# Moving three scatters to the end of a head pair, and the writing of empty rows into the second pair

## The chip, the cores and the metric

The kernel runs on one core of one Trainium2 chip. The metric is the device time of one execution in microseconds (us); of several executions the median counts.

## The reference

Attention with a hash mask, and then a mixture of experts on its result. For 4 batches, 8 heads, 768 positions and head size 64, queries and keys get a 6-bit bucket from the signs of a projection, and a query sees only the keys of its own bucket:

```python
q_bits = (np.einsum('bhsd,dk->bhsk', q, proj) > 0).astype(np.int64)
mask = q_bucket[:, :, :, None] == k_bucket[:, :, None, :]
scores = np.where(mask, scale * np.matmul(q, k.transpose(0, 1, 3, 2)), -1000000000.0)
attn = softmax(scores)
attn_out = np.matmul(attn, v)
```

The 3072 rows of 512 numbers that come of it go to one of 8 experts each, the one with the largest gate logit; a row's result is its gate weight times `np.maximum(x @ w1[e], 0.0) @ w2[e]`.

## The kernel before

**Stages.** The attention runs over 16 pairs of heads, g = 0 to 15 (four pairs to a batch). In a pair, TensorE makes 12 score tiles of 128 x 768 (line 300 the main product, line 298 one with the low parts of q and k and the mask bits), VectorE takes the row peaks (line 310), ScalarE the exponentials (line 316), and the tiles are transposed: four pairs of tiles by VectorE in 32 x 32 blocks (line 362), after which 16 DMAs put the blocks in their places (line 369, tensors z to pt), the other two on TensorE (line 330). In the next pair TensorE multiplies with v (lines 403 and 417), and lines 458 and 468 bring the result to token rows, xr, with the gate logits beside them. Once a batch is done, `route` finds expert and row number (slot) of each token in small steps, and the rows are scattered to a DRAM tensor `sorted_rows` that has a region for each expert. The experts' matmuls (lines 876, 915, 949) then read regions of that tensor with the load sizes fixed in advance; rows that no token fills must hold an empty row (zeros and a row number out of range), so `fill` writes 512 empty rows to the head of each of the 8 regions, ahead of the scatters.

**Order.** The order of the work is written out by hand: PLAN, NEXT, LAST and HEAD are strings of short step names, and `step` runs them one after the other, for the pairs 1 to 13, 14, 15 and 0. Each engine takes its instructions in that order, in one row per engine. What matters here: G is the projection for the hash bits (line 255), P0 to P7 prepare the next pair's q and k on GpSimd (`split`: P0, P1, P4 and P5 casts, lines 191 to 197; P2, P3, P6 and P7 low parts, lines 199 and 201), B writes the mask bits to DRAM and N reads them back (lines 266 and 271, issued by GpSimd), D0 to D3 are the block transposes, I and U the loads of q, k and v, V0 and V2 the two halves of the product with the block-transposed tiles (line 403, 24 matmuls a half), and C is one scatter.

**Scatters.** `scatter(b, hf)` is a generator for half of a batch: it copies the token numbers (line 584), and then issues three indirect DMAs from GpSimd, one for 128 rows each, with a small memset on a "spacer" ahead of each (lines 586 and 587). Each C in a pair runs it on by one DMA, in the pairs that WHEN names: 7 and 8 for batch 0, 11 and 12 for batch 1, 14 for the first half of batch 2.

**Fills.** `fill(e)` is one DMA of 1156 KB, issued by SP, for region e (line 148). The first six read one row of zeros in SBUF over and over, fills 6 and 7 copy the first region's rows in DRAM. Fills 0 to 3 stand in pair 0, at the steps z0 and z1 (the mask reads for pair 1); one more stands behind the 16 DMAs of the pairs 1, 2, 3 and 4 each (`blocks`, line 372). SP is the queue of all loads: q, k, v, the pt copies, later the weights.

Of the kernel before, what the change touches and what calls it, by code (L numbers as in the profile page):

```python
# [15 lines left out]
B, H, S, D = 4, 8, 768, 64  # L16
# [11 lines left out]
RW = GC + 2  # L28
# [14 lines left out]
FILL = 512  # L43
# [11 lines left out]
def lsh_attention_moe(ctx, tc, qk, qk2, v, proj, wg, w1, w1p, w2, w2p, out):  # L55
# [8 lines left out]
    xs = nc.dram_tensor("sorted_rows", [E * ROW, RW], F32).ap()  # L64
# [72 lines left out]
    C = {}  # L137
# [8 lines left out]
    def fill(e):  # L146

        nc.sync.dma_start(xs[e * ROW:e * ROW + FILL].rearrange("(p j) w -> p j w", p=128),
                          C["empty"][:, 0:1].to_broadcast([128, FILL // 128, RW]) if e < 6 else
                          xs[:FILL].rearrange("(p j) w -> p j w", p=128))  # L150

    def late_consts():
        tri = const.tile([128, 128], BF16, name="tri")
# [182 lines left out]
    def pt_tile(u):  # L336
        if u % 2 == 0:
            if "t" not in PT:
                PT["t"] = wk.tile([128, 4, 4, 2, NT, 32], F32, name="pt", bufs=1)
            PT[u] = PT["t"]  # L340
        elif u not in PT:
            PT[u] = wk.tile([128, 4, 2, 2, NT, 32], F32, name="pq", bufs=1)
        return PT[u]

    def turned(g):

        return 0 if g in (0, NG - 1) else 3 if g == NG - 2 else 4

    ZT = {}
    FILLS = {1: (4,), 2: (5,), 3: (6,), 4: (7,)}  # L350

    def blocks(g, c):

        if g not in ZT:
            ZT[g] = (moe.tile([128, 4, 3, 2 * NT * 32], F32, name="w0") if g == NG - 2 else
                     zp.tile([128, 4, 4, 2 * NT * 32], F32, name=f"z{g % 2}")), []
        z, n = ZT[g]
        n.append(c)
        i = 12 * g + 2 * c
        del PP[i], PP[i + 1]  # L360
        e = EP.pop(i // 2).rearrange("p s h c -> p (s h c)").rearrange("p (k g j) -> p g k j", g=4, j=32)
        nc.vector.transpose(z[:, :, c].rearrange("p g (k i) -> p g k i", i=32), e)  # L362
        if len(n) == turned(g):
            pt = pt_tile(2 * g)[:, :, :turned(g)]
            for h in range(2):
                for k in range(8):
                    x, j, y = k // 4, k // 2 % 2, k % 2
                    a, q = h + 2 * (x ^ y), (h ^ j) + 2 * y
                    nc.sync.dma_start(pt[32 * q:32 * q + 32, a].rearrange("p t s k i -> p (t s k i)"),
                                      z[32 * a:32 * a + 32, q].rearrange("p c x -> p (c x)"))  # L370
            del ZT[g]
            for e in FILLS.get(g, ()):
                fill(e)

    def trans_ev(c, k, vec):

# [356 lines left out]
    P2 = {}  # L733
# [66 lines left out]
    def tokens(n):  # L800
        r, o, c = PH[n]
        IX[n] = moe.tile([128, 4], I32, name="ix", bufs=3)
        t = len(tiles_of(c))
        nc.vector.tensor_copy(IX[n][:, :t], XG[n][:, :t, XG[n].shape[2] - 1].bitcast(I32))
# [204 lines left out]
    def weight_half(op, x):  # L1009
# [28 lines left out]
    PLAN = """  # L1038
        S1 P1 S0 Z1 G R1 S3 T30- Z1 R0 T51- T31- Z1 H T50- R3 Z1 S2 X0 E51v- S4 E31a- P3 T52- E50a- R2 T32- X1 S8 R4 D0
        A2 S5 X3 R5 E32a- M0- E30a- Z2 B S9 X2 R8 E52a- Z2 X4 V1- P4 P0 S6 Z2 D1 S7 R9 Z2 N R6 X8 V0- V2- O1- R7 X5 A1  # L1040
        Z1 X6 X7 I X9 D2 P5 D3 C O0- U Z2 T41 S11 E41a R11 T40 E40a K0- S10 L0- T42 P2 K1- X11 P7 P6 A0 R10 X10 L1-
        E42a C C
    """.split()

    NEXT = """
# [48 lines left out]
    def step(g, w):  # L1094
# [27 lines left out]
        elif op == "D":  # L1122
            if int(x) < turned(n):
                blocks(n, int(x))
# [78 lines left out]
    for g in range(NG):  # L1203
        if g == NG - 2:
            turn.close()
            late["p"] = ctx.enter_context(tc.tile_pool(name="late", bufs=1, side="right", reuse_waits="tile"))
        for w in HEAD if g == 0 else LAST if g == NG - 1 else NEXT if g == NG - 2 else PLAN:
            step(g, w)
            if g == 0 and w in ("z0", "z1"):
                fill(2 * int(w[1]))  # L1210
                fill(2 * int(w[1]) + 1)
            if g == NG - 1 and w == "c1":
                GT[0] = moe.tile([128, 4], F32, name="gate", bufs=3)
                nc.vector.tensor_copy(GT[0][:, :2], XG[0][:, :, GC])
                tokens(0)
# [60 lines left out]
    with tc.If(C["n"] > 0):  # L1276
        with tc.For_i(0, C["n"], 1) as i:
# [16 lines left out]
            p = ps.tile([128, 512], F32, name="t", bufs=2)  # L1294
# [5 lines left out]
            for f in range(8):  # L1300
                p = ps.tile([128, 512], F32, name="t", bufs=2)
# [3 lines left out]
            p = ps.tile([128, 512], F32, name="s", bufs=3)  # L1305
# [35 lines left out]
```

## Time and profile before

| | |
|---|---|
| timed runs | 692.9, 694.75 and 698.5 us; median 694.75 |
| the profiled execution | 690.59 us |
| its span, first to last instruction | 688.8 us |
| TensorE clock granted, mean | 0.994 |
| busy: TensorE, VectorE, ScalarE, GpSimd | 673.6, 468.1, 408.3, 467.8 us |
| moved by DMA | 136.94 MB, 199 GB/s in the mean |

The profiled execution is a single one, with 1.8 us around its span. Its engines are PE (TensorE matmuls), PEld (its weight loads), DVE (VectorE), ACT (ScalarE), POOL (GpSimd) and SP (SyncE, which here issues DMAs); "SPq" is an instruction that issues, not one that works. Times are us from the span's start.

### The profile page before, as it was taken

To read this page: it belongs to the slowest core of one execution; us is meant where nothing else is said; L and a number is where in the kernel's file an instruction comes from. 1 tells how busy PE (TensorE), PEld (TensorE's weight loads), DVE (VectorE), ACT (ScalarE), POOL (GpSimd) and SP (SyncE) were. 2 spreads that over 40 slices of the span, in tenths; PEclk is the share of its full clock that TensorE was granted. 3 is DMA by queue.
4 is the path that set the end of the run, shared out by engine and by line. 5 is a ranking of instruction groups with operands and counts; after the bars stand their busy time and mean duration, and the time that the engine had idled before them with its cause. 6 is when DMAs were issued, how large, how long until landed. Compare 5 with 4: busy or idle time off the path is not lost.

```text
span 688.8 us, 12591 instructions
## 1 busy us (share of the span) xinstructions
PE 673.6 (98%) x4383; PEld 568.0 (82%) x4383; DVE 468.1 (68%) x888; ACT 408.3 (59%) x810; POOL 467.8 (68%) x523
## 2 busy tenths in 40 slices
PE   9899999999999999989999999999999999999997
PEld 5777887778777887767787789899999999989896
DVE  8899889998899889968975653552453635352561
ACT  7887787877876787757685314643444444433410
POOL 7967575877778786776866346765567584949722
PEclk9999999999999999989999999999999999999999
DMA  8829999997879878995982239476638474757313
GB/s 301 285 53 262 287 257 280 268 259 198 229 225 277 217 194 220 268 252 152 264 274 88 92 131 276 150 202 150 189 127 220 157 204 157 212 191 204 127 12 43
DMA packets 72593, 136.94 MB, mean 199 GB/s; under 512 B 16353, under 2 KB 37089, under 8 KB 72464
## 3 DMA queue, kind: packets, MB, share of 16 engines
q1 hardware_dynamic: 64800, 117.00, 60.1%
q0 software_dynamic: 7584, 19.10, 9.5%
q8 instruction: 35, 0.57, 0.4%
q14 instruction: 30, 0.25, 0.2%
q10 hardware_dynamic: 144, 0.02, 0.0%
HBM read 65.75 MB, written 26.33 MB: 134 GB/s over the span
## 4 chain that ended last, share of the span: by engine, by line
PE 70%; POOL 12%; DMA 9%; issue 4%; SPq 2%; DVE 1%; ACT 1%; POOLq 0%; ACTq 0%
PE s L876 17%; PE s L915 11%; PE t L403 8%; PE s L949 7%; PE s L298 7%; PE s L300 6%; PE t L417 5%; PE t L330 5%; DMA masks<-bits 3%; PE t L458 2%; POOL w L772 2%; DMA sorted_rows<-xr,slot 2%; PE t L255 1%; SPq L933 1%; DMA w<-masks 1%
## 5 line engine op out<-in xcount | busy, mean ns | idle before, releaser
L316 ACT ACTIVATE e<-e,m 128x768 f32<-128x768 f32 x192 | 178.2, 930 | 39.7 <-DVE e L310 38.5
L310 DVE TENSOR_SCALAR_CACHE_REDUCE e<-s 128x768 f32<-128x768 f32 x192 | 178.0, 945 | 32.2 <-PE s L300 21.5
L772 POOL TENSOR_TENSOR w<-raw,w 128x512 fp32r<-128x512 f32 x112 | 142.4, 1299 | 33.4 <-ACT w L771 32.8
L876 PE MATMUL s<-xh,w 128*128 128x456 f32 (+6 forms) x672 | 124.0, 345 | 0.0
L876 PEld LDWEIGHTS s<-xh,w 128*128 128x128 f32 x672 | 119.9, 188 | 3.3 <-DVE xh L829 0.2
L892 DVE SCALAR_TENSOR_TENSOR hh<-s,hh 128x256 fp32r<-128x256 f32 (+7 forms) x64 | 35.5, 555 | 95.2 <-ACT hh L890 95.2
L362 DVE STREAM_TRANSPOSE z<-e 128x1536 f32<-128x1536 f32 x52 | 90.7, 1764 | 0.0
L403 PE MATMUL t<-pt,vt 128*64 128x256 f32 x720 | 81.2, 381 | 0.2 <-issue 0.2
L771 ACT ACTIVATE w<-raw 128x512 fp32r<-128x512 f32 x112 | 66.4, 623 | 18.4 <-DMA raw<-in_w1p_dram 18.4
L915 PE MATMUL s<-hh,w 128*128 128x456 f32 (+3 forms) x384 | 74.6, 355 | 0.0
L915 PEld LDWEIGHTS s<-hh,w 128*128 128x128 f32 x384 | 71.3, 188 | 2.7
L403 PEld LDWEIGHTS t<-pt,vt 128*64 128x64 f32 x720 | 50.6, 137 | 27.7 <-issue 3.3
L330 PE MATMUL t<-ident,e 128*128 128x128 f32 x492 | 71.2, 276 | 1.3 <-DVE pt L392 0.5
L890 ACT ACTIVATE hh<-s 128x256 fp32r<-128x256 f32 (+7 forms) x64 | 31.3, 490 | 67.5 <-PE s L876 66.3
L330 PEld LDWEIGHTS t<-ident,e 128*128 128x128 f32 x492 | 57.7, 140 | 12.3 <-issue 3.5
L298 PE MATMUL s<-w 80*128 80x384 f32 x192 | 56.0, 373 | 5.3 <-POOL spacer L586 3.7
L949 PE MATMUL s<-w,hh 128*128 128x512 f32 (+1 forms) x240 | 56.5, 395 | 0.9 <-DVE hh L892 0.9
L298 PE MATMUL s<-qk 80*128 80x384 f32 x192 | 54.5, 366 | 0.3 <-POOL spacer L586 0.2
L949 PEld LDWEIGHTS s<-w,hh 128*128 128x128 f32 (+1 forms) x240 | 44.6, 187 | 11.8 <-DVE hh L892 1.2
L394 ACT ACTIVATE pq<-t 128x512 f32<-128x512 f32 x75 | 44.1, 590 | 14.2 <-PE t L330 13.7
L300 PE MATMUL s<-w 128*128 128x384 f32 x192 | 50.5, 344 | 0.0
L300 PE MATMUL s<-qk 128*128 128x384 f32 x192 | 49.8, 340 | 0.0
(231 smaller groups left out, 1043.4 us busy)
## 6 DMA issues: line engine op xcount, KB each, us to landing
pt<-z SPq DMA_DIRECT2D x208, 192.0 KB
raw<-in_w1p_dram SPq DMA_DIRECT2D x28, 512.0 KB
xd<-in_qk_dram SPq DMA_DIRECT2D x14, 768.0 KB
raw<-in_w_dram SPq DMA_DIRECT2D x18, 512.0 KB
raw<-in_w2p_dram SPq DMA_DIRECT2D x16, 512.0 KB
sorted_rows<-xr SPq DMA_DIRECT2D x6, 1156.0 KB
vt<-in_v_dram SPq DMA_DIRECT2D x16, 384.0 KB
masks<-bits POOLq DMA_DIRECT2D x14, 192.0 KB
```

The costliest lines, as they stand in the source:

```text
L298: nc.tensor.matmul(p[:, a, :HALF], k[0:80, 2, c], k[0:80, 3, n], start=i >= 4, stop=i < 4)
L300: nc.tensor.matmul(p[:, a, :HALF], k[:, 0, c], k[:, 1, n], start=i < 4, stop=i >= 4)
L310: nc.vector.tensor_scalar(e, SC.pop(i)[:, :, :HALF], CEIL, None, op0=OP.min, op1=OP.min, accum_out=m)
L316: nc.scalar.activation(e, e, AF.Exp, bias=m, scale=-1.0, accum_out=SM[g][:, 3 * hf + t, s:s + 1])
L330: nc.tensor.transpose(o[:, j, w], e[w][:, kt // 3, (kt % 3) * 128:(kt % 3) * 128 + 128], ident)
L362: nc.vector.transpose(z[:, :, c].rearrange("p g (k i) -> p g k i", i=32), e)
L403: nc.tensor.matmul(PV[u][s * 64:(s + 1) * 64].rearrange("p (t b a i) -> p a t b i", t=4, b=2, a=2)[:, h], VT[g][:, kt, s, :], PT[u][:, h:: ...
L771: nc.scalar.activation(w[:, 0, a], r, AF.Copy)
L772: nc.gpsimd.tensor_tensor(w[:, 1, a], r, w[:, 0, a], op=OP.subtract)
L876: nc.tensor.matmul(p[:, :c], w[:, a, d, fs], x[:, b, d, :c], start=(k == 0), stop=(k == 11))
L915: nc.tensor.matmul(p[:, :c], w[:, a, f % 4, ms], h[b][:, f, :c], start=(k == 0), stop=(k == 23))
L949: nc.tensor.matmul(p[:pw], HH[n][b][:, f, i:i + pw], w[:, a, f % 4], start=(k == 0), stop=(k == 23))
```

## The change

Two things. In PLAN the first C moves from behind D3 to the end, so that all three scatters of a pair stand behind its last steps, P7 and P6 among them. And the fills stand elsewhere: two in pair 0, four in pair 1 at the steps S3, H, S4 and S9, one behind D3 in the pairs 2 and 3 each; all eight read SBUF.

```diff
     def fill(e):

         nc.sync.dma_start(xs[e * ROW:e * ROW + FILL].rearrange("(p j) w -> p j w", p=128),
-                          C["empty"][:, 0:1].to_broadcast([128, FILL // 128, RW]) if e < 6 else
-                          xs[:FILL].rearrange("(p j) w -> p j w", p=128))
+                          C["empty"][:, 0:1].to_broadcast([128, FILL // 128, RW]))
...
-    FILLS = {1: (4,), 2: (5,), 3: (6,), 4: (7,)}
+    FILLS = {(1, "S3"): 2, (1, "H"): 3, (1, "S4"): 4, (1, "S9"): 5, (2, "D3"): 6, (3, "D3"): 7}
...
             del ZT[g]
-            for e in FILLS.get(g, ()):
-                fill(e)
...
-        Z1 X6 X7 I X9 D2 P5 D3 C O0- U Z2 T41 S11 E41a R11 T40 E40a K0- S10 L0- T42 P2 K1- X11 P7 P6 A0 R10 X10 L1-
-        E42a C C
+        Z1 X6 X7 I X9 D2 P5 D3 O0- U Z2 T41 S11 E41a R11 T40 E40a K0- S10 L0- T42 P2 K1- X11 P7 P6 A0 R10 X10 L1- E42a
+        C C C
...
             if g == 0 and w in ("z0", "z1"):
-                fill(2 * int(w[1]))
-                fill(2 * int(w[1]) + 1)
+                fill(int(w[1]))
+            if (g, w) in FILLS:
+                fill(FILLS[g, w])
```

GpSimd's row in pair 7, from the mask reads for pair 8 to the last scatter, before (L195 and L197 are casts, L199 and L201 the low parts of q and k; the pairs 8, 11 and 12 read alike):

```order
L271 DMA qk<-masks 16x4x384 x2
L195 CAST qk<-xd 64x768
L197 COPY qk<-qk 64x768
L584 COPY xr<-tokid_i 128x3
L586 MEMSET spacer 1x1
L587 DMA sorted_rows<-xr,slot 25600x578
L199 TENSOR_TENSOR qk<-xd,qk 64x768
L201 TENSOR_TENSOR qk<-xd,qk 64x768
L199 TENSOR_TENSOR qk<-xd,qk 64x768
L586 MEMSET spacer 1x1
L587 DMA sorted_rows<-xr,slot 25600x578
L586 MEMSET spacer 1x1
```

The same place in the changed kernel (the line numbers have moved up by 1 to 3):

```order
L270 DMA qk<-masks 16x4x384 x2
L194 CAST qk<-xd 64x768
L196 COPY qk<-qk 64x768
L198 TENSOR_TENSOR qk<-xd,qk 64x768
L200 TENSOR_TENSOR qk<-xd,qk 64x768
L198 TENSOR_TENSOR qk<-xd,qk 64x768
L581 COPY xr<-tokid_i 128x3
L583 MEMSET spacer 1x1
L584 DMA sorted_rows<-xr,slot 25600x578
L583 MEMSET spacer 1x1
L584 DMA sorted_rows<-xr,slot 25600x578
L583 MEMSET spacer 1x1
```

The copy, the spacer and the DMA of the first scatter have moved from ahead of the three low parts to behind them. A little further in GpSimd's row of the changed kernel, at the start of pair 8, with what each instruction waits for (DMASW are the slots of GpSimd's own DMAs, the others engines):

```order
L1151 TENSOR_SCALAR xd<-xd 128x768 [waits PE_49]
L264 TENSOR_SCALAR bits<-bits,wsg 64x384 [waits Activation_49]
L265 DMA masks<-bits 128x384 [waits Pool_49]
L190 CAST w_2312<-xd 64x768 [waits DMASW3_49,DMASW7_49,DMASW1_49,DMASW0_49]
L192 COPY w_2312<-w_2312 64x768 [waits Pool_49]
```

The wait for all three scatters (slots 7, 0 and 1) stands at the cast behind the mask write; before, the slots 1 and 0 stood there, and slot 7 at the second of the three low parts.

SP's row in the first four pairs, before (xd are q and k, vt is v):

```order
L266 DMA masks<-bits 128x384
L148 DMA sorted_rows<-xr 512x1x578 x4
L81 DMA xd<-in_qk_dram 128x1536
L369 DMA pt<-z_506 32x1536 x16
L148 DMA sorted_rows<-xr 512x1x578
L85 DMA vt<-in_v_dram 128x768
L81 DMA xd<-in_qk_dram 128x1536
L369 DMA pt<-z_756 32x1536 x16
L148 DMA sorted_rows<-xr 512x1x578
```

And in the changed kernel, with what each one waits for (DMAHW are the slots of SP's DMAs):

```order
L265 DMA masks<-bits 128x384 [waits DMAHW3_49,Pool_49]
L148 DMA sorted_rows<-xr 512x1x578 [waits DMAHW4_49]
L148 DMA sorted_rows<-xr 512x1x578 [waits DMAHW5_49]
L148 DMA sorted_rows<-xr 512x1x578 [waits DMAHW6_49]
L148 DMA sorted_rows<-xr 512x1x578 [waits DMAHW7_49]
L148 DMA sorted_rows<-xr 512x1x578 [waits DMAHW0_49]
L148 DMA sorted_rows<-xr 512x1x578 [waits DMAHW1_49]
L81 DMA xd<-in_qk_dram 128x1536 [waits DMAHW2_49,DVE_49,PE_49]
L368 DMA pt<-z_507 32x1536 [waits DMAHW3_49,DVE_49,PE_49]
```

Six fills now stand in a row, ahead of the load of q and k for pair 3; between them SP waits for slots alone.

## Rows read from the trace of the kernel before

**Rows 1.** The page's first part: busy time, share of the span, instructions.

```profile
PE 673.6 (98%) x4383; PEld 568.0 (82%) x4383; DVE 468.1 (68%) x888; ACT 408.3 (59%) x810; POOL 467.8 (68%) x523
```

**Rows 2.** Windows: stretch, length, busy by engine (instructions), PEclk, DMA share, GB/s.

```profile
0.00:29.50 29.50, 25.74 (x151) 17.41 (x152) 24.68 (x68) 24.23 (x49) 24.87 (x36) 1.00 0.94 317
30.13:52.07 21.94, 21.94 (x165) 17.27 (x164) 19.82 (x33) 17.66 (x35) 15.35 (x16) 1.00 0.24 70
52.08:74.05 21.97, 21.97 (x165) 17.31 (x164) 19.82 (x34) 17.36 (x35) 13.37 (x15) 1.00 1.03 268
...
275.13:301.24 26.11, 23.49 (x166) 18.43 (x165) 21.26 (x37) 17.35 (x34) 19.88 (x24) 0.93 0.90 253
301.24:324.71 23.47, 23.47 (x166) 18.13 (x165) 19.37 (x34) 17.21 (x34) 18.27 (x22) 0.93 0.65 188
```

**Rows 3.** TensorE's timeline, pair ends: start, us, line, operation, [idle before, releaser].

```profile
183.46 0.62 PE L298 MATMUL s<-qk 80*128 80x384 f32 x2 [0.20 <-POOL spacer L586]
...
206.80 0.62 PE L298 MATMUL s<-w 80*128 80x384 f32 x2 [1.11 <-POOL spacer L586]
...
210.81 0.60 PE L298 MATMUL s<-w 80*128 80x384 f32 x2
...
298.38 1.01 PE L298 MATMUL s<-w 80*128 80x384 f32 x2 [2.62 <-POOL spacer L586]
...
305.14 0.59 PE L298 MATMUL s<-w 80*128 80x384 f32 x2
```

**Rows 4.** Windows of one us, behind the wait of 2.62 us.

```profile
299.00:300.00 1.00, 1.00 (x5) 1.00 (x4) 0.00 (x0) 0.00 (x0) 0.78 (x3) 0.50 1.06 252
```

**Rows 5.** GpSimd's timeline, end of pair 12.

```profile
287.41 0.83 POOL L197 CAST w<-w 64x768 fp32r<-64x768 f32 x1
...
294.75 1.81 POOL L201 TENSOR_TENSOR w<-xd,w 64x768 fp32r<-64x768 f32 x1 [2.74 <-DMA sorted_rows<-xr,slot]
296.53 1.80 POOL L199 TENSOR_TENSOR w<-xd,w 64x768 fp32r<-64x768 f32 x1
```

**Rows 6.** GpSimd's timeline, last pair: the third of three scatters in a row.

```profile
395.12 0.96 POOL L587 DMA_INDIRECT sorted_rows<-xr,slot  x1 [0.23 <-issue]
```

**Rows 7.** SP's timeline: the 16 pt copies of the pairs 7, 8, 10, 11, 12.

```profile
179.64 13.90 SPq L369 DMA_DIRECT2D pt<-z  x16
...
202.55 15.84 SPq L369 DMA_DIRECT2D pt<-z  x16
...
248.29 12.07 SPq L369 DMA_DIRECT2D pt<-z  x16
...
269.95 14.07 SPq L369 DMA_DIRECT2D pt<-z  x16
...
292.60 13.26 SPq L369 DMA_DIRECT2D pt<-z  x16
```

**Rows 8.** TensorE's timeline: V0 and V2 in the pairs 8, 9, 12, 13.

```profile
195.94 5.40 PE L403 MATMUL t<-pt,vt 128*64 128x256 f32 x48
...
222.30 2.81 PE L403 MATMUL t<-pt,vt 128*64 128x256 f32 x24 [0.19 <-issue]
...
286.01 5.40 PE L403 MATMUL t<-pt,vt 128*64 128x256 f32 x48
...
313.63 5.40 PE L403 MATMUL t<-pt,vt 128*64 128x256 f32 x48
```

**Rows 9.** Fills and masks, pairs 0 and 1: SP, the chain, TensorE, GpSimd.

```profile
13.31 4.19 SPq L148 DMA_DIRECT2D sorted_rows<-xr  x4
19.88 8.53 DMA w<-masks
28.55 0.59 PE L298 MATMUL s<-w 80*128 80x384 f32 x2 [1.57 <-DMA w<-masks]
49.62 0.82 POOL L195 CAST w<-xd 64x768 fp32r<-64x768 f32 x1 [5.23 <-PE s L300]
```

**Rows 10.** The scatters' line: duration in ns, least, median, most; first and last start.

```profile
L587 POOL DMA_INDIRECT sorted_rows<-xr,slot x24: 963/1000/1092, 174.4 to 402.4; - x24
```

## The prediction

> **What bounds the kernel now.** I read the page's head first: TensorE is busy 98% of the 688.8 us span [rows 1], so only its idle time, a lowered clock or fewer matmuls can shorten the kernel, and the change removes no matmul. Then the windows of single pairs (counted from 0, each from its projection matmuls, line 255, to those of the next): pair 1 takes 21.94 us at granted clock 1.00 with TensorE busy throughout, pairs 12 and 13 take 26.11 and 23.47 us at 0.93 [rows 2]. Two clean pairs are 2 x 21.94 = 43.88, so 5.70 us are lost there. Then the TensorE timeline at the ends of the pairs: the first scores of the next pair wait 0.20 us at 183.46, 1.11 us at 206.80 and 2.62 us at 298.38 [rows 3], each time until GpSimd has finished something ("POOL spacer" is what stands behind it there). These are the ends of pairs 7, 8 and 12. At the fourth end with a scatter (pair 11, near 273) no such row stands. After 298.38 the granted clock is 0.50 [rows 4], the 1.2 GHz level, where TensorE had stood still for 2.62 us; from the first score pair at 298.38 to the fifth one at 305.14 it needs 6.76 us, and the same steps one pair after the wait at 206.80 take 210.81 - 206.80 = 4.01 us at full clock [rows 3]: the clock costs 2.75 us. 2.62 + 2.75 = 5.37 is nearly the whole 5.70 of the two windows.
>
> Why GpSimd is late is in its timeline: in pair 12 the cast of line 197 ends at 288.24, but the low part of line 201 starts only at 294.75, having waited 2.74 us for the scatter's DMA, and the last low part (line 199, 296.53) ends at 298.33, 0.05 us before TensorE goes on [rows 5]. So a chain of scatter, landing, two low parts sets the end of the pair.
>
> **The change part by part.** *The scatters.* The first of three is moved behind the three low parts P2, P7, P6, together with its token copy, spacer and DMA; nothing is added or removed, and no other queue is touched. A scatter's turn on GpSimd is 0.96 us and 0.23 ahead of it, 1.2 us, where three stand in a row [rows 6]. In pair 12 the low parts would follow the cast at once: 288.24 + 1.83 + 1.81 + 1.80 = 293.7 (durations from [rows 5], the first taken like its sister's), while TensorE asks at 298.38 - 2.62 = 295.76. The 2.62 us go, with 2.1 us to spare, and with them the clock's 2.75. In pairs 7 and 8 the move takes at least one turn of 1.2 us from before the low parts, more than the 0.20 and 1.11 us waited. Gain: 2.62 + 1.11 + 0.20 + 2.75 = 6.68 us. On GpSimd the wait for the scatters moves to the first cast of the next pair (the order shows it waiting on all three); the last of three would end near 293.7 + 0.2 + 3 x 1.2 = 297.5, before the second one even began until now (after 298.33), so what is queued behind that cast comes no later than before.
>
> What is late next is the transposed blocks' copy pt, the 16 DMAs that SP issues from the end of D3, on which the second half of the P·V matmuls (V2, line 403) waits in the next pair. SP's run of 16 lasts 12.07 us in pair 10, which has no scatter, but 13.90, 15.84, 14.07 and 13.26 us in pairs 7, 8, 11 and 12 [rows 7]. After the run of pair 8, which ends at 218.39, V2 starts at 222.30, having waited 0.19 us [rows 8]: so V2 can start some 3.9 us after a run's end. Before, two scatters are issued inside the run and one ahead of it; now three stand at its beginning. What one scatter costs the run is not shown alone. Its bounds: 13.26 with three met (the first was still in flight at 292.60, since its landing released line 201 at 294.75) is (13.26 - 12.07) / 3 = 0.40 us each; 15.84 with two is 1.89 each. I take 0.95, by 13.90 and 14.07 (1.8 and 2.0 for two), so runs of 12.07 + 3 x 0.95 = 14.9 us. V2 may then start at 179.64 + 14.9 + 3.9 = 198.4 in pair 8, against 195.94 + 2.64 = 198.6 (half of the x48 row, less the 0.2 gained) [rows 8]: no wait to speak of. Pair 9: 202.55 + 18.8 = 221.35 against 222.11 - 1.31 = 220.8: 0.55. Pair 12: 288.75 against 286.01 + 2.64 = 288.65: 0.1. Pair 13: 292.60 + 18.8 = 311.4 against 313.63 + 2.64 - 5.37 = 310.9: 0.5. Less the 0.19 waited already, 1.0 us is given back. With 0.40 each it is nothing, and the 0.19 goes too: a gain of 6.9.
>
> *The empty rows.* Two of eight fills leave the first pair's code and stand in the second; the two that copied from DRAM now read SBUF. But SP waits for nothing of the second pair: in its row the six stand back to back and wait on DMA slots alone. SP issues four in 4.19 us from 13.31 [rows 9], so the six go out by about 20 us, two of them ahead of the load of pair 3's q and k, and their 2 x 1156 KB fall into the second pair, whose DMA share is 0.24 [rows 2]. I cost this at nothing: pairs 2 to 4, which four fills share now, are no longer for it: pair 2 takes 21.97 us at a DMA share of 1.03 [rows 2]. The cover is GpSimd's idle time: in the second pair its mask write meets traffic that was not there, but GpSimd sits idle 5.23 us at 49.62 waiting for TensorE's scores [rows 9]; a later landing under that costs nothing, one above it costs the excess. Bounds: 0 and a loss of 2.3 us (two fills' 2.37 MB at the first pair's 317 GB/s [rows 2] take 7.5 us, less 5.23).
>
> A rule of the Trainium skill speaks against putting scatters where VectorE is busy. All 24 scatter instructions take 963 to 1092 ns on GpSimd [rows 10], wherever they stand, so I count them as above. The page "SBUF — State Buffer", section "🔬 SBUF: two separate sides", says that a GpSimd-issued DMA starves for descriptors while a VectorE copy in a two-port mode holds the shared port pair, and its next section tells of about 620 ns turned into about 3100. By it the three turns could stretch to some 15 us, an estimate from that page, and most of the gain would be lost again; the row does not bear it out, so it has no chance of its own.
>
> Sum: 6.68 - 1.0 = 5.7 us. The profiled execution took 690.59 us (span 688.8 and 1.8 around it), so 684.9 by its own time. The three timed runs lie at 692.9, 694.75 and 698.5, all above it; nothing shows where their extra time is. On the median: 694.75 - 5.7 = 689.0 us.
>
> **The rivals.** *More of the same.* The runs above the profiled one may be longer by the same waits (a wait at pair 8 or 11 that also lowers the clock costs 2.75 more). For it: the waits hang on landings that differ by us from pair to pair. Against: not seen. With the full 6.9 and half of the 4.16 us between profile and median, 694.75 - 9.0 = 685.8.
>
> *The pt copies take most of it back.* At 1.3 us per scatter the runs are 16.0, 1.1 longer than I take; four V2 waits of up to 1.1 more and the first 1.0 make 5.2: 1.5 us gained, 693.2. For it: the run of 15.84 and that V2 already waits after it.
>
> *The pt copies decide, and it is slower.* Same place. At 1.89 us per scatter a run is 17.7 and V2 waits 2.9 (pair 8), 3.4, 2.9 and 3.3 us: 12.5, that is 5.6 more than is gained with the old 0.19 off, and where a wait is like the 2.62 us after which the clock fell, 2.75 each: up to 11 more. Time 700 to 711. It decides from waits of 6.68 / 4 = 1.7 us each, which is some 1.4 us per scatter. For it: pair 8. Against: 13.26 to 14.07 in three of four.
>
> *The fills hold up the first masks.* Mask reads issued by 19.88 share the DMA engines with the fills, and TensorE waits 1.57 us for them at 28.55 [rows 9]. If they had to wait out two more fills, 7.5 us and the clock's 2.75 come on top: 694.75 - 5.7 + 10.2 = 699. Against: they landed 8.53 us after 19.88 [rows 9], at 28.4, though four fills and a load had been issued by then, and the DMA share of the first pair is 0.94 to its end at 29.5 [rows 2]: they did not wait for the fills' queue to run dry.
>
> *It does not do what it says.* The fills are not paced by the second pair's steps (above); that costs nothing by itself, and the forecast has it in.
>
> **How the numbers follow.** Forecast (687.5 to 691.5): 0.47. More of the same: 0.27. pt takes most: 0.12. pt decides, slower: 0.09. Masks: 0.05. A measurement of this kernel tells about 1% from no change, that is 687.8 and 701.7 here. Below 687.8 lie nearly all of the second case and a seventh of the first: 0.34. Above 701.7 most of the slower pt case: 0.07. Within: 0.59. The range reaches from 683.5, the second case with some more, to 695.5, past the case in which pt takes all; beyond it lie the two slower ones and a little below: under 0.2.
>
> **What would show it.** Right: no TensorE row waits on GpSimd at the ends of pairs 7, 8 and 12, the low part behind P2 (line 200 there) waits for no scatter, pairs 12 and 13 at about 22 us each and clock 1.00. Right on pt: the runs near 14.9 us, V2 waiting 0.5 us in pairs 9 and 13. Right on the fills: six issued between 13 and 20 us, the second pair's DMA share well above 0.24, its length still 21.9. Wrong: idle rows over 1.7 us before V2, a low clock in pairs 8 to 13, or a longer wait than 1.57 us on the masks near 28 us.

## The result, and the profile after

| | before | after |
|---|---|---|
| median, us | 695.32 (692.9 to 700.84, 6 executions) | 686.57 (684.69 to 692.44, 6 executions) |
| ratio, 95% interval | | 0.9899 (0.9859 to 0.994) |
| the profiled execution, us | 690.59, span 688.8 | 686.28, span 684.4 |
| mean granted clock of it | 0.994 | 0.999 |

The changed kernel is about 1% faster; the forecast was 689.0 us, worked out from the first three executions of the kernel before (median 694.75). (A ratio is formed over undisturbed executions, so it need not be the quotient of two medians.) Measured once more with other kernels it had 689.34 and 0.9921. The page's first part, against [rows 1]: TensorE is busy 3.1 us less, with as many matmuls, because the clock stayed up (2.75 of the 3.1 us, by the ledger below).

```profile
PE 670.5 (98%) x4383; PEld 565.7 (83%) x4383; DVE 472.9 (69%) x888; ACT 408.6 (60%) x810; POOL 466.9 (68%) x523
```

The windows of the pairs 1, 2, 8, 12 and 13 after (columns as in [rows 2]):

```profile
30.29:52.26 21.97, 21.97 (x166) 17.31 (x165) 19.32 (x33) 17.67 (x35) 16.01 (x16) 1.00 0.65 190
52.26:74.23 21.97, 21.97 (x165) 17.32 (x164) 19.82 (x34) 17.36 (x35) 15.55 (x16) 1.00 0.79 212
184.73:208.50 23.77, 22.18 (x165) 17.23 (x165) 19.92 (x35) 17.35 (x35) 19.31 (x23) 1.00 0.94 258
275.04:298.28 23.24, 22.20 (x165) 17.22 (x165) 19.98 (x35) 17.36 (x35) 18.16 (x22) 1.00 0.95 266
298.28:321.31 23.03, 22.24 (x165) 17.40 (x164) 20.24 (x36) 17.61 (x36) 17.64 (x21) 1.00 0.85 228
```

Pairs 12 and 13 took 26.11 and 23.47 us at clock 0.93; now 23.24 and 23.03 at 1.00. They are still not the 22 us of a clean pair, and pair 8 is one of 23.77. Pair 1 keeps its 22 us while its DMA share goes from 0.24 to 0.65. TensorE's timeline says where the pairs 8, 12 and 13 lose time. The first scores at the ends of the pairs 7, 8 and 12 no longer wait, in place of [rows 3]; V2 does, in the pairs 8 and 12 (in [rows 8] it stood unbroken behind V0 there), and one wait at the end of pair 13 is new:

```profile
183.14 0.60 PE L297 MATMUL s<-qk 80*128 80x384 f32 x2
...
200.00 2.81 PE L400 MATMUL t<-pt,vt 128*64 128x256 f32 x24 [1.58 <-DMA pt<-z]
...
206.90 0.61 PE L297 MATMUL s<-w 80*128 80x384 f32 x2
...
289.78 2.81 PE L400 MATMUL t<-pt,vt 128*64 128x256 f32 x24 [1.04 <-DMA pt<-z]
...
296.68 0.61 PE L297 MATMUL s<-w 80*128 80x384 f32 x2
...
319.69 0.62 PE L297 MATMUL s<-qk 80*128 80x384 f32 x2 [0.79 <-POOL qk L198]
```

The last row is the one at the end of pair 13, which has no scatter: there TensorE waits for a low part of GpSimd. The same wait stands in "fills only" below (0.59 us), whose scatters are where they were, and not in "scatters only" and "after again", so the move of the scatters does not bring it; what does is not shown.

SP's timeline, the 16 pt copies of the pairs 7, 8, 10, 11 and 12, against [rows 7]:

```profile
179.77 15.43 SPq L368 DMA_DIRECT2D pt<-z  x16
201.74 14.30 SPq L368 DMA_DIRECT2D pt<-z  x16
...
248.43 11.91 SPq L368 DMA_DIRECT2D pt<-z  x16
270.18 14.60 SPq L368 DMA_DIRECT2D pt<-z  x16
292.10 13.93 SPq L368 DMA_DIRECT2D pt<-z  x16
```

GpSimd's timeline at the end of pair 12, against [rows 5]: the three low parts follow one another without a break and end at 290.64 instead of 298.33, and the scatters come behind.

```profile
284.23 0.82 POOL L196 CAST w<-w 64x768 fp32r<-64x768 f32 x1
285.12 1.83 POOL L198 TENSOR_TENSOR w<-xd,w 64x768 fp32r<-64x768 f32 x1
287.01 1.83 POOL L200 TENSOR_TENSOR w<-xd,w 64x768 fp32r<-64x768 f32 x1
288.80 1.84 POOL L198 TENSOR_TENSOR w<-xd,w 64x768 fp32r<-64x768 f32 x1
...
294.13 0.96 POOL L584 DMA_INDIRECT sorted_rows<-xr,slot  x1 [0.22 <-issue]
```

Fills and masks, against [rows 9]: SP's fills, TensorE's first wait for masks and low parts (here the row names GpSimd's low part, which ends at 28.58; the second mask read landed at 28.57), and GpSimd in pair 1.

```profile
14.18 7.63 SPq L148 DMA_DIRECT2D sorted_rows<-xr  x6
21.92 6.19 SPq L81 DMA_DIRECT2D xd<-in_qk_dram  x1
28.70 0.59 PE L297 MATMUL s<-w 80*128 80x384 f32 x2 [0.83 <-POOL w L198]
41.11 1.03 POOL L270 DMA_DIRECT2D qk<-masks  x2 [4.82 <-DMA masks<-bits]
49.82 0.82 POOL L194 CAST w<-xd 64x768 fp32r<-64x768 f32 x1 [0.37 <-PE s L299]
```

**The ledger of the two profiles.** The pairs 7 to 13 took 162.06 us (162.65 to 324.71) and take 158.54 (162.77 to 321.31): 3.52 less. The waits of [rows 3], 3.93 us, the clock's 2.75 and V2's old 0.19 are gone, 6.87 together; given back are 1.58 + 1.04 + 0.79 = 3.41. That leaves 3.46, which is the 3.52. From pair 14 on it is another 1.0 us (364.1 to 363.1): one wait of 0.91 us in the experts is gone, which the change does not touch, so that part is put down to chance here. Pair 7 starts 0.1 later.

### The profile page after: what moved, and what is told of

The parts are those of the page before. It is cut to its first block, busy times and chain, and to the rows that moved or that the text cites. A ratio compares the mean times of both kernels' runs of the same rounds, so it can differ in the third digit from the quotient of the medians.

```text
span 684.4 us, 12592 instructions
## 1 busy us (share of the span) xinstructions
PE 670.5 (98%) x4383; PEld 565.7 (83%) x4383; DVE 472.9 (69%) x888; ACT 408.6 (60%) x810; POOL 466.9 (68%) x523
## 4 chain that ended last, share of the span: by engine, by line
PE 77%; POOL 7%; DMA 4%; DVE 4%; SPq 4%; issue 3%; ACT 1%; POOLq 0%; DVEq 0%
PE s L873 21%; PE s L912 11%; PE s L946 10%; PE t L400 8%; PE s L297 7%; PE s L299 6%; PE t L414 5%; PE t L329 5%; SPq L368 4%; DMA pt<-z 3%; PE t L455 2%; DMA masks<-bits 2%; DVE z L361 1%; DVE e L309 1%; POOL qk L198 1%
## 5 line engine op out<-in xcount | busy, mean ns | idle before, releaser
L769 POOL TENSOR_TENSOR w<-raw,w 128x512 fp32r<-128x512 f32 x112 | 142.5, 1299 | 33.4 <-ACT w L768 31.9
L768 ACT ACTIVATE w<-raw 128x512 fp32r<-128x512 f32 x112 | 66.4, 623 | 13.6 <-DMA raw<-in_w1p_dram 13.5
L946 PEld LDWEIGHTS s<-w,hh 128*128 128x128 f32 (+1 forms) x240 | 44.5, 187 | 11.0 <-ACT hh L887 0.4
```

The source lines that it names most:

```text
L768: nc.scalar.activation(w[:, 0, a], r, AF.Copy)
L769: nc.gpsimd.tensor_tensor(w[:, 1, a], r, w[:, 0, a], op=OP.subtract)
L946: nc.tensor.matmul(p[:pw], HH[n][b][:, f, i:i + pw], w[:, a, f % 4], start=(k == 0), stop=(k == 23))
```

## The experiments

All medians in one table, and where one profiled execution of each spent its time (from the first matmul of line 255, or 254, of one pair to that of another; "to 1" is pair 0 with what is ahead of it):

| kernel | median (executions) | ratio (95%) | to 1 | 1, 2 | 3 to 6 | 7 to 13 | rest |
|---|---|---|---|---|---|---|---|
| before | 695.32 (6) | 1 | 30.1 | 43.9 | 88.6 | 162.1 | 364.1 |
| after | 686.57 (6) | 0.9899 (0.9859–0.994) | 30.3 | 43.9 | 88.5 | 158.5 | 363.1 |
| scatters only | 692.35 (12) | 0.9948 (0.9918–0.9978) | 32.8 | 46.5 | 88.7 | 156.5 | 363.2 |
| fills only | 695.73 (12) | 0.9979 (0.9946–1.0011) | 30.5 | 43.9 | 91.0 | 162.3 | 363.7 |
| four pairs without scatters | 688.21 (4) | 0.9891 (0.9839–0.9943) | 31.9 | 44.5 | 88.1 | 154.0 | 364.6 |
| all fills first | 688.97 (4) | 0.9868 (0.9817–0.992) | 30.9 | 43.9 | 88.4 | 162.4 | 364.3 |
| after again | 689.34 (8) | 0.9921 (0.9882–0.9961) | 30.7 | 44.8 | 91.0 | 156.1 | 364.8 |
| scatter ahead of P6 | 699.19 (10) | 1.0065 (1.0029–1.0101) | 32.0 | 44.3 | 88.5 | 167.7 | 363.3 |
| two scatters a pair | 686.17 (6) | 0.9863 (0.9823–0.9903) | 30.9 | 43.9 | 92.1 | 157.4 | 365.1 |
| "no fill in pair 0" | 708.5 (4) | 1.0216 (1.0153–1.0279) | 32.2 | 46.3 | 107.2 | 158.1 | 362.8 |
| scatter ahead of P2 | 684.09 (4) | 0.9823 (0.9779–0.9868) | 30.7 | 43.9 | 88.0 | 156.4 | 363.4 |
| one, two, three scatters | 690.31 (1) | | 30.5 | 43.9 | 88.7 | 157.2 | 368.1 |
| fills first, two a pair | 686.68 (6) | 0.9842 (0.9795–0.9889) | 30.5 | 43.9 | 88.1 | 157.9 | 363.9 |
| ahead of P2, fills first | 686.72 (6) | 0.9887 (0.9845–0.9928) | 32.4 | 44.4 | 88.1 | 154.6 | 366.1 |

A single profile moves by several us in stretches that an edit does not touch (the experts' rest alone from 362.8 to 368.1). So a stretch is read here by its named waits, and a kernel by its median.

**The two parts, each alone.** The PLAN of the diff above in the kernel before:

> The kernel before with the scatters moved to the end of the pair and the fills left as they were. Theory (the landing of the first scatter stood on GpSimd's way to the low parts, and cost TensorE 3.9 us of waiting and 2.75 us of clock; the fills are worth nothing): ratio to before 0.990 (0.986 to 0.994), as with both edits; no TensorE wait on GpSimd at the ends of pairs 7, 8 and 12, clock 1.00 in pairs 12 and 13. Rival (the DMA time that the fills take from pairs 2 to 4 is what counts): ratio 0.997 to 1.003.

and the fills of the changed kernel with the old PLAN:

> The changed kernel with the scatters put back where they were, the fills as changed. Theory: ratio to before 0.997 to 1.003, the wait of some 2.6 us at the end of pair 12 and the low clock behind it are there again. Rival (the fills count): ratio about 0.990, and the pairs 2 to 4 shorter than 21.9 us.

The scatters alone bring half a per cent (1% was expected), the fills alone nothing that their interval tells from zero, and both together 0.8 to 1.0. The intervals of the scatters alone and of both overlap. In the profiles the pairs 7 to 13 go with the scatters: 156.5 against 162.3 us. With the fills alone the old wait stands at the end of pair 12, and the clock falls behind it. TensorE's timeline:

```profile
301.72 0.96 PE L297 MATMUL s<-w 80*128 80x384 f32 x2 [2.31 <-POOL spacer L583]
```

A window of one us behind it (the clock is the third number from the end, as in [rows 4]):

```profile
302.00:303.00 1.00, 1.00 (x4) 1.00 (x4) 0.00 (x0) 0.00 (x0) 1.00 (x2) 0.50 1.08 258
```

With the scatters alone the same happens in another place, the first wait for masks. TensorE's timeline:

```profile
30.01 0.98 PE L298 MATMUL s<-w 80*128 80x384 f32 x2 [2.33 <-DMA w<-masks]
```

And the window there:

```profile
30.00:31.00 1.00, 0.99 (x3) 1.00 (x4) 0.00 (x0) 0.00 (x0) 1.00 (x1) 0.50 1.05 407
```

Pair 2 starts at 57.2 there and at 52.3 in the changed kernel. The mean granted clock over the executions fits this: 0.992 before (23), 0.994 with either part alone (12 each), 0.999 (6) and 0.998 (8) with both. 0.6% of 688 us is 4 us.

**What the scatters still cost.** The changed kernel with the scatters of the pairs 7, 8, 11 and 12 left out:

```diff
-    WHEN = {7: (0, 0), 8: (0, 1), 11: (1, 0), 12: (1, 1), 14: (2, 0)}
+    WHEN = {14: (2, 0)}
```

> The changed kernel with the four groups of scatters of the pairs 7, 8, 11 and 12 left out, so the rows of the batches 0 and 1 never reach the experts. Theory (each scatter that meets SP's run of 16 pt copies lengthens it by about 0.9 us, and V2 waits for the copies): the runs of those four pairs last 11.5 to 12.3 us, V2 waits nowhere, pairs 8 and 12 take about 22.0 us, and the time is 2 to 3.5 us under the changed kernel's (ratio to before 0.984 to 0.988). Rival (other traffic, the masks and loads, lengthens the runs): runs still 14 us and more, V2 still waits 1 us and more in pairs 8 and 12.

The pairs 7 to 13 take 154.0 us, and TensorE waits nowhere in them: 4.5 us less than after, 8.0 less than before. That is the floor of this stretch. The runs of pt copies in the pairs 7, 8, 11 and 12 are 12.15, 11.57, 12.34 and 10.95 us, mean 11.75. The median does not show the 4.5 us. In the profile the first wait for masks was 1.61 us and the clock fell behind it, which makes the time up to the end of pair 2 some 2.2 us longer than after, and the rest is 1.5 us longer; what the other executions lost is not shown.

**The fills moved to the front.** Four at z0 and four at z1 of pair 0, FILLS empty:

```diff
-                fill(int(w[1]))
+                for e in range(4):
+                    fill(4 * int(w[1]) + e)
```

> The changed kernel with all eight fills in pair 0's code, so that SP issues eight in a row instead of six. Theory (SP is not paced, and the fills' traffic is covered by GpSimd's idle time at the end of pair 1, of which 0.4 us was left with six): the mask write of pair 1 lands about 7 us later than 40.8, TensorE waits 5 to 7 us for GpSimd near 50, the clock falls behind it, and the time is 6 to 10 us above the changed kernel's (ratio to before 0.998 to 1.005). The masks of pair 0 land as before, near 28.5. Rival one (the queues share so that the mask write is not held up): no new wait, ratio 0.990. Rival two (mask reads wait out the whole queue of fills): TensorE waits 7 us and more near 28.

TensorE's waits of the first 60 us hold 1.3 us for the masks, and the pairs 3 to 6 are clean; eight fills at once cost nothing that shows, as the first rival had it. The loss of this profile is elsewhere, and it makes the pairs 7 to 13 as long as before (162.4 us): a wait for GpSimd's low part at the end of pair 13, like the one above, and V2 again, this time also for v, whose load SP issues behind the pt copies. The clock fell behind the two of 2.4 us.

```profile
PE s L297 <- POOL qk L198: 2.4, 1, 2.4
PE t L400 <- DMA vt<-in_v_dram: 2.4, 1, 2.4
PE t L400 <- DMA pt<-z: 1.3, 1, 1.3
```

**The changed kernel again**, beside the next three:

> The changed kernel once more, beside the three variants. Theory of the two covers: both idle stretches that could pull TensorE's clock down are gone (2.62 us at the end of pair 12; the mask wait of pair 0, 0.84 us instead of 1.57 to 2.33), so that the mean granted clock of its executions is 0.998 to 1.000 and the median 685 to 688 us, and in pairs 8 and 12 V2 waits for the pt copies again, 1 to 1.6 us each. Rival (the fills' new places do nothing, only the scatters count): clock as in the run with the scatters' move alone, 0.992 to 0.996, median 690 to 693.

The clock came as expected, 0.998 in the mean, the median 1.3 us above the expected. In its profile only one V2 wait is left (0.8 us), but the pairs 3 to 6 take 91.0 us: at the ends of the pairs 4 and 5 TensorE waits for GpSimd and the masks (its waits from 97 to 146 us: in all, times, longest), and GpSimd, in its own row, for the load of q and k.

```profile
PE s L297 <- POOL qk L198: 1.4, 1, 1.4
PE s L297 <- DMA w<-masks: 1.0, 1, 1.0
```

```profile
119.34 0.82 POOL L194 CAST qk<-xd 64x768 fp32r<-64x768 f32 x1 [3.46 <-DMA xd<-in_qk_dram]
```

Waits like these stand in the profiles of "fills only", "two scatters a pair" and "no fill in pair 0" too, and in none of the five whose fills are all first or as before. Full DMA engines alone do not explain it: over the pairs 3 to 5 their share is 0.92 here, 0.81 with all fills first (the last kernel below), but 0.95 before, without a wait.

**Landing or turn: one scatter ahead of a low part.** First ahead of P6:

```diff
-T42 P2 K1- X11 P7 P6 A0 R10 X10 L1- E42a C C C
+T42 P2 K1- X11 P7 C P6 A0 R10 X10 L1- E42a C C
```

> The changed kernel with the first of the three scatters put back between P7 and P6: ahead of one low part, but of one that works on partitions 0 to 63 (even head), so that nothing of the odd head stands behind it before the next pair. Theory of the landing wait (what made the low parts late was the 2.74 us at P7 for the scatter's landing, which piled up over the pairs): P6 ends 1.35 us later than in the changed kernel (292.0 instead of 290.64 in pair 12), no idle time of GpSimd on sorted_rows ahead of it, TensorE never waits for it (it needs it 5 us later), time 685 to 689 us. Rival (the turn: any scatter ahead of a low part starves TensorE): waits of 1 to 2.6 us for GpSimd at the ends of the pairs 8 and 12 come back, and 690 to 693 us.

The expectation names P6 wrongly: `split` numbers P4 to P7 for the odd head, so P6 is one of its parts, and this run shows the opposite case. It is the slowest of the orders. GpSimd's timeline in pair 8:

```profile
205.57 1.07 POOL L584 DMA_INDIRECT sorted_rows<-xr,slot  x1 [0.56 <-POOL spacer L583]
211.39 1.79 POOL L198 TENSOR_TENSOR w<-xd,w 64x768 fp32r<-64x768 f32 x1 [4.75 <-DMA sorted_rows<-xr,slot]
```

TensorE's timeline at the end of the pair:

```profile
213.23 0.68 PE L297 MATMUL s<-w 80*128 80x384 f32 x2 [4.77 <-POOL spacer L583]
```

P6 waits 4.75 us for the scatter to land, and TensorE as long for P6; the pair takes 27.9 us. Then the same with P2, which is a part of the even head:

```diff
-T42 P2 K1- X11 P7 P6 A0 R10 X10 L1- E42a C C C
+T42 K1- X11 P7 P6 C P2 A0 R10 X10 L1- E42a C C
```

> The changed kernel with the low parts in the order P7, P6, P2 and the first scatter between P6 and P2. P2 works on the even head, so that GpSimd has a scatter's turn (1.35 us) ahead of a low part, but nothing that waits for the scatter's landing before the next pair. Theory of the landing wait: no idle time of GpSimd ahead of P2, P2 ends 1.2 to 1.5 us later than the last low part of the changed kernel (292 in pair 12), TensorE does not wait for it, median 685.5 to 690 us (the changed kernel had 686.57 and 689.34). Rival (the turn itself starves TensorE): waits of 1 us and more for GpSimd at the ends of the pairs 8 and 12, median 692 us or more.

```profile
288.45 1.06 POOL L584 DMA_INDIRECT sorted_rows<-xr,slot  x1 [0.57 <-POOL spacer L583]
289.54 1.83 POOL L198 TENSOR_TENSOR w<-xd,w 64x768 fp32r<-64x768 f32 x1
```

P2 starts 0.03 us behind the scatter, TensorE waits for no low part at the ends of the pairs 7, 8 and 12, and 684.09 us is the lowest median of all. One scatter's turn ahead of a low part costs nothing that shows. Its landing ahead of one costs 11.3 us in the pairs 7 to 13 of the two profiles (167.7 against 156.4); of the 15 us between the medians (699.19 against 684.09) 1.7 more stand at the first masks, behind which only the slower profile lost the clock. So the wait for the landing is what the change removed. The copies gain too: with one of the three scatters ahead of them their runs are 13.55 us in the mean of this kernel and 14.29 in that of the last one below (four each).

**How much a scatter lengthens the copies.** Two to a pair, and one, two and three (a table of pairs takes the place of WHEN):

```diff
+    DOSE = {6: (0, 0), 7: (0, 1), 8: (1, 1)}
...
+    DOSE = {6: (0,), 7: (0, 0), 8: (1, 1, 1)}
```

> The changed kernel with the twelve scatters of the first two batches two to a pair, at the end of the pairs 6, 7, 8 and 10, 11, 12, instead of three to a pair in 7, 8, 11, 12. Theory of the dose (a scatter lengthens the run of 16 pt copies beside it by 0.97 us, from 11.65 without one to 14.6 with three; V2 waits from a run of 13.6 on): runs of 13.2 to 13.9, V2 waits 0.5 us in all (2.63 in the changed kernel), pairs 6 to 13 take 178.0 to 178.8 us together (180.7 in the changed kernel), time 683 to 685.5 us. Rival (what delays the copies is there once for a pair with scatters, whatever their number, such as a load queued behind them): six runs of 14 us and more, V2 waits in four to six pairs, 3 to 6 us in all, 687 to 690 us.

> The changed kernel with one scatter at the end of pair 6, two at the end of 7, three at the end of 8, and the same in 10, 11, 12. Theory of the dose (0.97 us a scatter on top of 11.65): runs of the 16 pt copies of 12.6, 13.6 and 14.6 us, each within 0.8; V2 waits only in the pairs behind three, 0.7 to 1.3 us. Rival (a pair with scatters has a longer run whatever their number): the run beside one scatter is 14 us or more. Second rival (only the third one hurts, since the first two land before the run is under way): one and two leave the run under 12.5.

The runs of the second kernel beside one, two and three scatters, twice (SP's timeline):

```profile
158.44 12.56 SPq L368 DMA_DIRECT2D pt<-z  x16
180.08 14.92 SPq L368 DMA_DIRECT2D pt<-z  x16
202.11 13.42 SPq L368 DMA_DIRECT2D pt<-z  x16
...
248.43 13.14 SPq L368 DMA_DIRECT2D pt<-z  x16
270.08 12.90 SPq L368 DMA_DIRECT2D pt<-z  x16
292.19 15.27 SPq L368 DMA_DIRECT2D pt<-z  x16
```

Single runs scatter by over 1 us, so two of the six miss their 0.8 (14.92 and 13.42). V2 waits 1.5 us for v behind the 14.92 beside two scatters, which was not expected, and 0.9 behind three. Over all profiles with the scatters at the pair's end the means are 11.75 us with none (4 runs, "four pairs without scatters"), 12.85 with one (2), 13.94 with two (14), 14.79 with three (22): 1.0 us a scatter, nearly in a straight line. The step from runs to waits missed: two a pair leave V2 waiting 1.6 us for v and 0.4 for pt, and the profile's stretches are not shorter than with three. SP issues v's load behind the copies, so it is as late as they are.

**Fills out of pair 0.**

```diff
+    FILLS = {(1, "S3"): 0, (1, "H"): 1, (1, "S4"): 2, (1, "S9"): 3, (2, "D3"): 4, (3, "D3"): 5, (4, "D3"): 6, (5, "D3"): 7}
...
-                fill(int(w[1]))
```

> The changed kernel without the two fills of pair 0: regions 0 to 3 at the four places of pair 1, 4 to 7 behind D3 in the pairs 2 to 5. Theory (the mask read for the first score tiles of the next pair lands late because fills hold the DMA engines): the read lands 3 to 4 us after its issue instead of 8, TensorE's idle time before 30 us falls from 0.8 us and more to under 0.2, pair 1 starts 0.8 us earlier, 685 to 686.5 us. Rival (the loads of q, k and v fill the DMA engines there anyway): the read still takes 7 us and more, no gain, 686 to 688 us; and with two more fills beside pt copies, in pairs 4 and 5, up to 1 us of waits there.

It told something else. SP waits for nothing, so four fills went out at 13.6 us all the same, with the load of q and k at their heels, as before the change, and TensorE waited 2.20 us for the masks. The last fill, issued at 153.74, then ran into the scatters' tiles: the zeros that a fill reads lie in a tile of the kind `xr`, and VectorE could not use that memory until the last fill had landed. SP's timeline at the start:

```profile
13.61 4.19 SPq L148 DMA_DIRECT2D sorted_rows<-xr  x4
17.90 1.57 SPq L81 DMA_DIRECT2D xd<-in_qk_dram  x1
```

VectorE's wait for the fill in its timeline, and TensorE's longest wait from 140 to 186 us:

```profile
162.26 0.61 DVE L465 TENSOR_TENSOR xr<-t,r 128x432 f32<-128x432 f32 x1 [17.10 <-DMA sorted_rows<-xr]
```

```profile
PE t L329 <- DVE xr L465: 13.1, 1, 13.1
```

**Versions of the best parts.** Put together from the diffs shown above: fills first with two scatters a pair, and fills first with the scatter ahead of P2.

> All eight fills in pair 0, and two scatters at the end of the pairs 6, 7, 8, 10, 11, 12. Theory (the fills of pairs 1 to 3 keep the DMA engines full until 130 us and so delay the mask reads of pairs 3 to 5, by 2.4 to 3.6 us in three of the profiles; three scatters a pair make V2 wait, two don't): pairs 3 to 5 take 66.2 to 66.5 us, pairs 6 to 13 together 177.5 to 179.5, the span is 681.5 to 685, the median 682.5 to 685.5 us, below the changed kernel's. Rival (eight fills at once delay the first masks and copies by as much): TensorE idle for 2 us and more before 31 us, or pair 1 and 2 over 45 us together, and a median of 686 to 689.

> Two of the variants together: the low parts in the order P7, P6, P2 with the first scatter between P6 and P2 (684.09 us by itself), and all eight fills in pair 0. Theory (the two act in different places): TensorE idle for the masks 0.8 to 1.4 us before 31 us, pairs 3 to 5 take 65.8 to 66.4 us together, pairs 6 to 13 178 to 179, clock 0.997 to 1.000, median 682.5 to 685.5 us. Rival (what is gained is the choice of executions, not the order): median 686.5 us or more, as the changed kernel had in two sets.

Neither median is below 686, where 682.5 to 685.5 was expected of both: 686.68 and 686.72. Both clean the pairs 3 to 6 (88.1 us). In the first V2 still waits, 0.93 and 1.42 us for v, though only two scatters stand in a pair. In the second V2 does not wait and the pairs 7 to 13 take 154.6 us, 0.6 above the floor; it loses in the wait for the first masks (1.82 us, and the clock 0.50 behind it) and in the experts (366.1). The scatter ahead of P2 has the lowest median, 684.09 in four executions; the others have 686.2 to 689.3. But the second version keeps its order and came out as the rival of its expectation had it (686.5 or more: the gain is the choice of executions), and the interval of the order alone just meets that of the first measurement of the changed kernel (0.9868 and 0.9859). That it beats the changed kernel is not shown.

## Why the prediction held, and where it did not

**The scatters' gain: right, in every term.** No low part waits on a landing, no TensorE row on GpSimd at the ends of the pairs 7, 8 and 12, the clock is 1.00 behind them. The pair of runs with a scatter ahead of P6 and P2 shows the cause: the landing. The price that the prediction set on a turn, 1.2 us taken from before the low parts, was not what counted.

**The copies: the term of the run right, that of the wait mis-sized.** 0.95 us a scatter and runs of 14.9 were predicted; 1.0 and 14.79 are the means over all runs, 15.43, 14.30, 14.60, 13.93 in this profile. But V2 was to wait 1.15 us, 0.55 of it in pair 9, 0.1 in 12 and 0.5 in 13 (1.0 less the old 0.19), and it waited 2.62, in the pairs 8 and 12 (2.43 less the old 0.19). The step that failed is "V2 can start some 3.9 us after a run's end", read from one pair of before, whose row names no DMA as the releaser ([0.19 <-issue]). Here it started 4.8 us (200.00 - 195.20) and 5.0 us (289.78 - 284.78) after it. With 3.9 the same runs would have made V2 wait 0.68 and nothing. (The sum for pair 8 does not take off the 0.2 that it names: V2 asks at 198.4 and not 198.6, just when the copies allow it; this changes nothing.) In the pairs 9 and 13 the wait did not come: the one ahead had moved TensorE back by 1 to 1.6 us, the copies not. For the 0.79 us at the end of pair 13 the prediction has no term.

**The fills: costed at nothing, and both signs were wrong.** A gain was not among the bounds. Six fills ahead of the load of q and k push it behind the mask reads (issued at 21.92 after the change, the reads at 19.97 and 20.74; before, the load at 17.61 and the reads at 19.11 and 19.88). Where four fills and then the load go out (before and two of the runs), TensorE's first wait for masks is 1.57, 2.33 and 2.20 us; with six or eight fills first it is 0.83 to 1.82, 1.23 in the mean of eleven profiles. That the load's place makes the difference is likely by these rows, but three profiles stand against eleven. The clock fell behind it in two of the three and in four of the eleven. The loss is in another place: the cover named, GpSimd's 5.23 us, did hold the mask write's delay (4.82 of it were used, 0.37 left), but in three of the eight profiles with paced fills the pairs 3 to 6 take 2.3 us more and over; why in these three and not in the other five stays open ("no fill in pair 0", with waits of the same kind in the pairs 4 and 5, is not among the eight). So does what the fills are worth alone, since the interval of "fills only" holds no change; that the clock stays up only with both parts shows in the means over the executions.

**From the profile to the median.** 4.4 us less in the profiles and 8.7 in the first medians (6.4 in the second set) need not agree: the median of before, 695.32, lies 4.7 us above its profiled execution, that of after 0.3. The clock makes some 1.4 us of this, an estimate (0.992 in the mean against 0.994 in the profile, of 688 us); for the rest there is no profile. This was the rival "more of the same", with a chance of 0.27; the medians lie on both sides of the line between it and the forecast, and of its waits only the clock's part shows. The sum was 5.7 us; the profiles show 3.46 for its terms and 1.0 of chance in the experts, the medians 8.7 and 6.4. That the forecast of 689.0 came as near as it did is in part luck: too little was given back in it, and the executions of before ran longer than its profile.

**The page that spoke against it.** The Trainium skill, "SBUF — State Buffer", section "🔬 SBUF: two separate sides", would have the scatters starve beside VectorE. After the change, too, no turn is long (the scatters' line, as in [rows 10]). The row shows GpSimd's turns alone; the scatters landed 2.9 to 6.6 us after their start, and no run tells whether VectorE has a part in that.

```profile
L584 POOL DMA_INDIRECT sorted_rows<-xr,slot x24: 960/980/1088, 180.8 to 399.1; - x24
```

## What to carry to other kernels

Ask of each DMA that an engine issues not only how long the issue takes, but which next instruction of that engine waits for the landing: two orders that differ by the place of one low part were 11 us apart in the pairs concerned. Where TensorE has waits behind which its clock falls in some executions, a small change elsewhere decides several us, and only many executions tell it. Moving a transfer in the program's text moves it in time only if its queue waits for something there.

## What was not expected of the hardware

The clock fell behind single waits of 1.30, 1.45, 1.61 and 1.82 us, and did not behind others of 1.57, 1.58, 2.0 (pair 8 of "fills only") and 2.17 (pair 4 of "two scatters a pair"): from the length of one wait it cannot be told in this range. A DMA that GpSimd issues does not stand behind those of SP: with six fills under way that landed 14.9 us after their issue in the median, the mask reads landed after 7.9 while SP's own load of q and k behind the fills landed after 19.3 (issues of 10 to 45 us after the change; KB each, median us to landing):

```profile
sorted_rows<-xr SPq DMA_DIRECT2D x6, 1156.0 KB, 14.9
xd<-in_qk_dram SPq DMA_DIRECT2D x1, 768.0 KB, 19.3
w<-masks POOLq DMA_DIRECT2D x2, 96.0 KB, 7.9
```

The Trainium skill, "DMA: Bandwidth & Descriptors", section "🔬 SWDGE vs HWDGE vs iDMA", says that each DMA engine goes round between the queues of the two kinds; these rows agree. And what a scatter costs beside the copies is some 1.0 us each, in place of the 0.40 to 1.89 that one profile left open.
